# Forgetting attention and a SwiGLU FFN on one core: attention by query block, the FFN fed in 128-token blocks, transposes by DMA, and one planned order for all engines

## The chip, the cores and the metric

The kernel runs on one NeuronCore of a Trainium2 chip. The core has TensorE (PE, matrix products, whose weight loads the profile lists as PEld), VectorE (DVE), ScalarE (ACT), GpSimd (POOL), and SyncE (SP), which here only issues DMAs. Sixteen DMA engines move data between HBM and the on-chip SBUF. Matrix products land in PSUM, which has eight banks of 128 partitions x 512 fp32. The metric is the device time of one execution in microseconds (us); smaller is better.

## The reference, cut to what matters

q, k and v are 8 batches x 8 heads x 576 tokens x 64 in fp32; f is one forget gate per token and head. The FFN weights are 512 x 1536 (gate and value) and 1536 x 512 (out).

```python
scores = scale * np.matmul(q, k.transpose(0, 1, 3, 2))
log_f = np.log(np.clip(f, 0.0001, 1.0))
cum = np.cumsum(log_f, axis=-1)
decay = cum[:, :, :, None] - cum[:, :, None, :]
causal = np.triu(np.ones((S, S), dtype=bool), k=1)
scores = np.where(causal, -1000000000.0, scores + decay)
...
attn = attn / (np.sum(attn, axis=-1, keepdims=True) + 1e-09)
return np.matmul(attn, v).astype(np.float32)
...
xn = x / rms * rms_g
g = xn @ w_gate
silu = g * (1.0 / (1.0 + np.exp(-g)))
val = xn @ w_val
return (silu * val @ w_out).astype(np.float32)
```

x is the attention output with the eight heads side by side: 4608 tokens x 512, so one batch is 576 rows of x, which is four blocks of 128 tokens and one of 64.

## The kernel before

**Attention.** A batch b goes through the same steps. `load_qk` (line 73) issues ten casting DMAs on POOL's queue (fp32 in HBM to bf16 in SBUF; line 77), one per 128-token block of q and of k. `load_v` (line 83) issues five on SP's. `transposes` (line 163) turns q and k on TensorE: per pair of heads five 128x128 transposes into one PSUM tile `tr`, then a DVE copy (line 169); 40 transposes a batch. `scale_v` (line 155) multiplies v by the decay factor on POOL and appends the factor as a 65th column, so that the same product gives the denominator. `scores` (line 194) works head by head: a head's whole causal triangle fills three PSUM banks of 512 columns (`BANKS`), a matmul contracts over 64 rows, head 2p in partitions 0 to 63 and head 2p+1 in 64 to 127, each bank is exponentiated by one ACT instruction of 128x512 (line 205), and POOL masks the diagonals (lines 208 and 213). `scores4` (line 171) does the last 64x64 corner of all heads. `values` (line 225) makes 15 matmuls of 65 columns for a head, all five query blocks, and DVE divides (lines 234 and 235). Only when all eight heads are done are the batch's five blocks of x complete. Then `norm` (line 240) takes the squares on ACT (245), the power on POOL (249), the scaling on DVE (252), and `transpose_x` (line 254) turns the batch's xn in 20 TensorE transposes and copies them into `xT` with the gain (265).

**FFN.** Groups of 512 tokens, so nine groups that straddle batches. `gate(g, fc)` (line 290) does four gate matmuls of 512 columns, tanh on ACT, a DVE product (301), four value matmuls, a second DVE product (306); twelve of these a group. `project(g, j)` (line 308) does twelve matmuls for 128 tokens, an ACT copy and a store on SP; four a group. Three PSUM banks `ff` serve both.

**Order.** Each engine runs its instructions in program order. The loads of weights, of batch 1 and of `wo` are issued behind batch 0's loads, all of batch 0's attention comes first (lines 331 and 332), and then a loop over the FFN's 144 pieces interleaves the attention of batches 1 to 7, by costs written beside each piece, with a lead of six pieces:

```python
for work in ffn:
    n += 1
    want = lead + total_a * n / (slots + LEAD)
    while i < len(stream) and done_a < want:
        done_a += stream[i][0]
        stream[i][1]()
        i += 1
    work[1]()
```

Of the kernel before, what the change touches and what calls it, by code (L numbers as in the profile page):

```python
# [8 lines left out]
F32 = mybir.dt.float32  # L9
# [14 lines left out]
def kernel(  # L24
    ctx: ExitStack,
    tc: tile.TileContext,
    q: bass.AP,
    k: bass.AP,
    v: bass.AP,
    f: bass.AP,  # L30
    moe_w_gate: bass.AP,
    moe_w_val: bass.AP,
    moe_w_out: bass.AP,
    moe_rms_g: bass.AP,
    out: bass.AP,
):
# [4 lines left out]
    NB = 5  # L41
    DM = moe_w_gate.shape[0]
    DF = moe_w_gate.shape[1]
    NDC = DM // 128
    NFC = DF // 128
    GT = 512
    n_grp = B * S // GT
    scale = 1.0 / (D ** 0.5)

    consts = ctx.enter_context(tc.tile_pool(name="consts", bufs=1))  # L50
    ldp = ctx.enter_context(tc.tile_pool(name="ldp", bufs=1))
    vp = ctx.enter_context(tc.tile_pool(name="vp", bufs=6))
    qkt = ctx.enter_context(tc.tile_pool(name="qkt", bufs=2))
    ptp = ctx.enter_context(tc.tile_pool(name="ptp", bufs=5))
    xp = ctx.enter_context(tc.tile_pool(name="xp", bufs=2))
    xnp = ctx.enter_context(tc.tile_pool(name="xnp", bufs=1))
    small = ctx.enter_context(tc.tile_pool(name="small", bufs=4))
    xtp = ctx.enter_context(tc.tile_pool(name="xtp", bufs=3))
    hp = ctx.enter_context(tc.tile_pool(name="hp", bufs=2))
    ep = ctx.enter_context(tc.tile_pool(name="ep", bufs=3))  # L60
    ps_tr = ctx.enter_context(tc.tile_pool(name="ps_tr", bufs=1, space=PSUM))
    ps_sc = ctx.enter_context(tc.tile_pool(name="ps_sc", bufs=3, space=PSUM))
    ps_o = ctx.enter_context(tc.tile_pool(name="ps_o", bufs=1, space=PSUM))
    ps_f = ctx.enter_context(tc.tile_pool(name="ps_f", bufs=3, space=PSUM))


    qb = [ldp.tile([128, NB, H * D], BF16, name=f"qb{i}") for i in range(2)]
    kb = [ldp.tile([128, NB, H * D], BF16, name=f"kb{i}") for i in range(2)]
    Vs = [ldp.tile([128, NB, H, D + 1], BF16, name=f"Vs{i}") for i in range(2)]
    PT4 = [[ldp.tile([128, 5 * 64], BF16, name=f"PT4_{i}{j}") for j in range(2)] for i in range(2)]  # L70


    def load_qk(b):
        for j in range(NB):
            p0, n = j * 128, min(128, S - j * 128)
            for src, dst in ((q, qb[b % 2]), (k, kb[b % 2])):
                nc.gpsimd.dma_start(  # L77
                    out=dst[0:n, j, :].rearrange("p (h d) -> p h d", d=D),
                    in_=src[b, :, p0:p0 + n, :].rearrange("h p d -> p h d"))

    v32s = {}

    def load_v(b):
        for j in range(NB):
            p0, n = j * 128, min(128, S - j * 128)
            v32 = v32s[b, j] = vp.tile([128, H, D], F32, name="v32")
            nc.sync.dma_start(out=v32[0:n, :, :],
                              in_=v[b, :, p0:p0 + n, :].rearrange("h p d -> p h d"))

    fr = consts.tile([BH, S], F32)  # L90
    nc.sync.dma_start(out=fr, in_=f.rearrange("b h s -> (b h) s"))

    for t in qb + kb:
        nc.vector.memset(t[64:128, NB - 1, :], 0.0)
    load_qk(0)
    load_v(0)
    for t in Vs:
        nc.vector.memset(t[64:128, NB - 1, :, :], 0.0)
    for pair in PT4:
        for t in pair:  # L100
            nc.vector.memset(t[:, 4 * 64:], 0.0)

    ident_f = consts.tile([128, 128], F32)
    make_identity(nc, ident_f)
    ident = consts.tile([128, 128], BF16)
    nc.vector.tensor_copy(ident, ident_f)

    rg = consts.tile([128, NDC], F32)
    with nc.allow_non_contiguous_dma(reason="512 gains, once"):
        nc.sync.dma_start(out=rg, in_=moe_rms_g.rearrange("(c p) -> p c", p=128))  # L110
    mhalf = consts.tile([128, NB], F32)
    nc.gpsimd.memset(mhalf, -0.5)


    wg = consts.tile([128, NDC, DF], BF16)
    wv = consts.tile([128, NDC, DF], BF16)
    wo = consts.tile([128, NFC, DM], BF16)

    def load_w(i):
        c0, c1 = i * 512, (i + 1) * 512  # L120
        for w, src in ((wg, moe_w_gate), (wv, moe_w_val)):
            nc.gpsimd.dma_start(out=w[:, :, c0:c1],
                                in_=src[:, c0:c1].rearrange("(c p) f -> p c f", p=128))

    def load_wo():
        for i in range(2):
            nc.gpsimd.dma_start(
                out=wo[:, i * 6:(i + 1) * 6, :],
                in_=moe_w_out[i * 768:(i + 1) * 768, :].rearrange("(c p) f -> p c f", p=128))


    nc.vector.tensor_scalar(fr, in0=fr, scalar1=1e-4, op0=ALU.max, scalar2=1.0, op1=ALU.min)
    nc.scalar.activation(fr, fr, ACT.Ln)
    one = consts.tile([BH, 1], F32)
    nc.vector.memset(one, 1.0)
    ones = bass.AP(tensor=one.tensor, offset=one.offset, ap=[one.ap[0], [0, S]])
    cum = consts.tile([BH, S], F32)
    nc.vector.tensor_tensor_scan(cum, ones, fr, 0.0, ALU.mult, ALU.add)
    mid = consts.tile([BH, 1], F32)
    nc.vector.tensor_tensor(mid, cum[:, 0:1], cum[:, S - 1:S], ALU.add)  # L140
    nc.vector.tensor_scalar_mul(mid, mid, 0.5)
    dec = consts.tile([BH, NB * 128], F32)
    nc.vector.memset(dec[:, S:], 0.0)
    nc.scalar.activation(dec[:, 0:S], cum, ACT.Exp, scale=-1.0, bias=mid[:, 0:1])
    decT = consts.tile([128, NB, BH], F32)
    for j in range(NB):
        dps = ps_o.tile([128, BH], F32, name="po")
        nc.tensor.transpose(dps, dec[:, j * 128:(j + 1) * 128], ident_f[0:BH, 0:BH])
        nc.vector.tensor_copy(decT[:, j, :], dps)


    QT, KT, PT = {}, {}, {}
    xs, xTs = {}, {}

    def scale_v(b):
        for j in range(NB):
            v32 = v32s.pop((b, j))
            n = min(128, S - j * 128)
            dj = decT[0:n, j, b * H:(b + 1) * H]
            nc.gpsimd.tensor_tensor(Vs[b % 2][0:n, j, :, 0:D], v32[0:n, :, :], bcast(dj, D), ALU.mult)  # L160
            nc.gpsimd.tensor_copy(Vs[b % 2][0:n, j, :, D], dj)

    def transposes(b, p):
        for src, store, nm in ((qb[b % 2], QT, "QT"), (kb[b % 2], KT, "KT")):
            tp = ps_tr.tile([128, NB * 128], BF16, name="tr")
# [214 lines left out]
```

## Time and profile before

| what | value |
|---|---|
| time, median of 3 runs | 486.65 us (486.64 to 487.0) |
| span of the profiled execution, first to last instruction | 484.0 us |
| around the span, median less span | 2.65 us |
| busy share PE, DVE, ACT, POOL | 88%, 54%, 46%, 39% |
| granted TensorE clock | 1.000 |
| bytes moved by DMA | 33.73 MB |

The profile shows one execution. The time of that execution outside the span is not listed; the table takes it from the median. A timeline row gives the start, the time that it covers, engine, line, output<-input, shape and count; in brackets stands the idle time of the engine before the row and what released it. Matmuls overlap in the pipeline, so a matmul's own duration (380 ns for 512 columns) is longer than the step from one start to the next; prices are taken from the steps. An SPq row is the time that SP's sequencer spent on issuing a DMA.

### The profile page before, as it was taken

The page shows a single profiled execution, that of the slowest core. Times are in us where ns is not written, and L with a number is a line of the kernel's source. Part 1 is how long each engine was busy: PE and PEld are TensorE (multiplying, and loading weights), DVE is VectorE, ACT ScalarE, POOL GpSimd, SP SyncE. Part 2 cuts the span into 40 slices and gives each one's busy share as a digit, 9 for nine tenths or more (in the row PEclk, how much of TensorE's full clock was granted, in tenths as well). Part 3 has the DMA queues.
Part 4 walks back from the last instruction along what each step waited for, and adds up shares of the span by engine and source line. Part 5 has one row for each costly group of instructions (what it writes and reads, how often), then busy time and mean ns, then how long its engine had stood idle before and what let it go on. Part 6 is the DMA issues. An engine that isn't in the chain of part 4 may idle for free.

```text
span 484.0 us, 8505 instructions
## 1 busy us (share of the span) xinstructions
PE 423.9 (88%) x3317; PEld 207.6 (43%) x3317; DVE 260.3 (54%) x534; ACT 222.1 (46%) x436; POOL 187.7 (39%) x335
## 2 busy tenths in 40 slices
PE   0491707999999999999999999999999999999996
PEld 0231403454544454445444544454444544444442
DVE  3210326478447844784478457745774577373670
ACT  3060321664465437544754474447444744232321
POOL 8539990665182518252825282513111211000000
PEclk9999999999999999999999999999999999999999
DMA  9999991594190419041903290010001000201102
GB/s 151 175 195 178 191 187 33 36 65 99 65 120 3 100 66 119 3 100 67 120 1 77 70 118 0 1 66 23 3 0 66 23 1 0 88 1 45 43 1 87
DMA packets 123080, 33.73 MB, mean 70 GB/s; under 512 B 113760, under 2 KB 118368, under 8 KB 123040
## 3 DMA queue, kind: packets, MB, share of 16 engines
q0 software_dynamic: 79744, 14.16, 36.6%
q1 hardware_dynamic: 43296, 19.03, 14.9%
q8 instruction: 26, 0.43, 0.4%
q14 instruction: 14, 0.11, 0.1%
HBM read 37.90 MB, written 9.44 MB: 98 GB/s over the span
## 4 chain that ended last, share of the span: by engine, by line
PE 67%; POOL 13%; issue 6%; DMA 6%; ACT 5%; DVE 2%; POOLq 0%; ACTq 0%
PE ff L311 20%; PE ff L296 14%; PE ff L304 13%; PE sc L202 7%; PE po L231 5%; PE tr L167 4%; DMA wv<-in_moe_w_val_dram 3%; PE tr L258 3%; POOL Vs_104 L160 2%; DMA qb_100<-in_q_dram 2%; ACT junk L245 2%; POOL Vs_105 L160 2%; POOL rs L249 2%; ACT PT L205 2%; POOL qb_100 L77 2%
## 5 line engine op out<-in xcount | busy, mean ns | idle before, releaser
L205 ACT ACTIVATE PT<-sc 128x512 bf16<-128x512 f32 x192 | 105.1, 599 | 87.6 <-PE sc L202 73.8
L296 PE MATMUL ff<-xT,wg 128*128 128x512 bf16 x432 | 114.7, 382 | 0.7 <-DVE xT L265 0.6
L304 PE MATMUL ff<-xT,wv 128*128 128x512 bf16 x432 | 114.0, 380 | 0.0
L311 PE MATMUL ff<-wo,hT 128*128 128x512 bf16 x432 | 112.5, 380 | 0.0
L301 DVE SCALAR_TENSOR_TENSOR ga<-th,ff 128x512 f32<-128x512 f32 x108 | 74.2, 687 | 66.9 <-ACT th L299 66.3
L299 ACT ACTIVATE th<-ff 128x512 f32<-128x512 f32 x108 | 64.5, 598 | 82.6 <-PE ff L296 80.9
L306 DVE SCALAR_TENSOR_TENSOR hT<-ga,ff 128x512 bf16<-128x512 f32 x108 | 74.2, 687 | 9.0 <-PE ff L304 0.3
L304 PEld LDWEIGHTS <-wv 128*128 128x128 bf16 x432 | 42.2, 98 | 50.2 <-issue 2.5
L208 POOL TENSOR_SCALAR_AFFINE_SELECT PT<-PT 128x128 bf16<-128x128 bf16 x64 | 19.1, 299 | 97.8 <-ACT PT L205 97.6
L296 PEld LDWEIGHTS <-wg 128*128 128x128 bf16 x432 | 38.6, 98 | 42.0 <-issue 5.6
L314 ACT COPY ores<-ff 128x512 f32<-128x512 f32 x36 | 21.1, 586 | 75.2 <-PE ff L311 74.4
L213 POOL TENSOR_SCALAR_AFFINE_SELECT PT<-PT 128x384 bf16<-128x384 bf16 x64 | 33.0, 528 | 53.2 <-ACT PT L205 53.1
L311 PEld LDWEIGHTS <-hT 128*128 128x128 bf16 x432 | 36.5, 98 | 36.4 <-issue 9.5
L231 PEld LDWEIGHTS <-PT 128*128 128x128 bf16 x896 | 35.7, 102 | 31.2 <-POOL PT L208 9.7
L234 DVE RECIPROCAL rden<-po 128x5 f32<-128x5 f32 x64 | 12.2, 191 | 55.3 <-PE po L231 55.3
L258 PE MATMUL tr<-ident,xn 128*128 128x128 bf16 x160 | 20.6, 229 | 18.3 <-DVE xn L252 18.0
L231 PE MATMUL po<-Vs_104,PT 128*128 128x65 bf16 x448 | 22.7, 206 | 13.6 <-POOL PT L208 9.2
L235 DVE TENSOR_TENSOR x<-po,rden 128x320 f32<-128x320 f32 x64 | 31.4, 490 | 1.7
L245 ACT ACTIVATE junk<-x 128x512 bf16<-128x512 f32 x40 | 25.0, 624 | 9.0 <-DVE x L235 8.4
L258 PEld LDWEIGHTS <-xn 128*128 128x128 bf16 x160 | 12.4, 100 | 37.0 <-DVE xn L252 29.1
L265 DVE TENSOR_SCALAR xT<-tr,rg 128x512 bf16<-128x512 bf16 (+7 forms) x64 | 20.5, 362 | 12.3 <-PE tr L258 12.1
L252 DVE TENSOR_SCALAR xn<-x,rs 128x512 bf16<-128x512 f32 x40 | 18.1, 520 | 13.2 <-POOL rs L249 13.2
(300 smaller groups left out, 387.8 us busy)
## 6 DMA issues: line engine op xcount, KB each, us to landing
out_dram<-ores SPq DMA_DIRECT2D x36, 256.0 KB, 2.0
qb_100<-in_q_dram POOLq DMA_DIRECT2D x16, 128.0 KB, 5.3
kb_102<-in_k_dram POOLq DMA_DIRECT2D x16, 128.0 KB, 5.4
qb_101<-in_q_dram POOLq DMA_DIRECT2D x16, 128.0 KB, 4.4
kb_103<-in_k_dram POOLq DMA_DIRECT2D x16, 128.0 KB, 4.5
wg<-in_moe_w_gate_dram POOLq DMA_DIRECT2D x3, 512.0 KB, 12.7
wv<-in_moe_w_val_dram POOLq DMA_DIRECT2D x3, 512.0 KB, 14.0
wo<-in_moe_w_out_dram POOLq DMA_DIRECT2D x2, 768.0 KB, 12.3
```

What stands on the lines that cost most here:

```text
L202: nc.tensor.matmul(sc[:, c:c + n], lhsT=KT[b, p][rows, kj * 128:(kj + 1) * 128], rhs=QT[b, p][rows, q0:q0 + n], start=True, stop=True)
L205: nc.scalar.activation(t[:, bank * 512:(bank + 1) * 512], sc, ACT.Exp, scale=scale)
L213: nc.gpsimd.affine_select(out=d, in_=d, pattern=[[0, 3], [1, 128]], compare_op=ALU.is_ge, fill=0.0, base=0, channel_multiplier=-1)
L231: nc.tensor.matmul(po[:, qi, :], lhsT=weights_of(b, h, qi, kj), rhs=Vs[b % 2][:, kj, h, :], start=(kj == 0), stop=(kj == qi))
L245: nc.scalar.activation(junk, x[:, j, :], ACT.Square, accum_out=sq[:, j:j + 1])
L258: nc.tensor.transpose(tp[:, j * 128:(j + 1) * 128], xn[:, j, dc * 128:(dc + 1) * 128], ident)
L296: nc.tensor.matmul(pg, lhsT=wg[:, dc, fc * 128:(fc + 1) * 128], rhs=xT[:, dc, :], start=(dc == 0), stop=(dc == NDC - 1))
L299: nc.scalar.activation(t, pg, ACT.Tanh, scale=0.5)
L301: nc.vector.scalar_tensor_tensor(a, in0=t, scalar=1.0, in1=pg, op0=ALU.add, op1=ALU.mult)
L304: nc.tensor.matmul(pv, lhsT=wv[:, dc, fc * 128:(fc + 1) * 128], rhs=xT[:, dc, :], start=(dc == 0), stop=(dc == NDC - 1))
L306: nc.vector.scalar_tensor_tensor(hTs[g][:, fc, :], in0=a, scalar=0.5, in1=pv, op0=ALU.mult, op1=ALU.mult)
L311: nc.tensor.matmul(po, lhsT=hTs[g][:, fc, j * 128:(j + 1) * 128], rhs=wo[:, fc, :], start=(fc == 0), stop=(fc == NFC - 1))
```

## The change

The kernel is rewritten around a plan that is made when the program is built. Every piece of work is a `Unit` with an engine, a duration written by hand, a priority key (lower goes first), the units that it depends on and the buffers (`Hold`) that it takes and gives back. `Plan.run` plays the units through in time: whenever an engine is free, the ready unit with the lowest key whose buffers are free starts. The order in which units started is the order in which the instructions are emitted, for all engines. Emission is under `tc.manual_schedule()`.

What the units are:

- **Attention by query block.** A score unit covers one or two tiles of a query block `qi` and a key block `kj`, for all eight heads at once: a tile is two PSUM banks (even heads and odd heads), filled by eight matmuls of 128 columns that alternate between the two row halves, one ACT exponential of 128x1024 and, on the diagonal, one POOL mask of 128x1024. The 64 tokens of the last block take two key blocks to a tile. A value unit is four heads of one query block, with a DVE division behind it. A block of x is complete when its query block is, and not when the batch is.
- **Norm by one or two blocks.** Squares on ACT, power on POOL, and one DVE operation for scale and gain. For batch 0's first four blocks TensorE turns xn, with a DVE copy. All other blocks (36) are turned by a DMA transpose on SP from SBUF to SBUF.
- **q and k.** The first four blocks of batches 0 and 1 are turned on TensorE (64 transposes); the other 64 blocks, each 128 (or 64) tokens x 512, by a DMA transpose on SP.
- **V** is scaled on DVE for batches 0 and 1, and on POOL for the others.
- **FFN.** Group g is now the first 512 tokens of batch g; the ninth is the eight 64-token remainders. Groups 0 and 1 are fed by 128-token blocks: one unit does four columns of fc for one block (16 matmuls of 128 columns for the gate, 16 for the value). The others do as before. The plan splits a projection in three units.
- **Buffers.** PSUM is two score tiles of two banks, one bank for the value product, three for the FFN; `tr` is gone, and once the last score is done its banks go to the FFN.

```diff
-LEAD = 6
+class Plan:
...
+            for eng, line in ready.items():
+                if busy.get(eng) or not line:
+                    continue
+                best = None
+                for u in line:
+                    if best is not None and u.key >= best.key:
+                        continue
+                    want = [h.ring for h in u.take if h.slot is None]
+                    if all(len(free[r]) >= want.count(r) for r in want):
+                        best = u
...
+                order.append(best)
...
+    def load(eng, issue, moves, key, emit, deps=(), take=(), give=()):
+
+        lane = Hold("hw" if eng == "SP" else "sw", 1)
+        u = P.add(eng, issue, key, emit, deps, list(take) + [lane], ())
+        return P.add("DMA", moves, key, None, [u], (), list(give) + [lane], lat=1.7)
...
+    LEAD, SPAN = 0.3, 0.85
+    def akey(b, w):
+        return b - 1 - LEAD + SPAN * w
...
+    load_w(0, -12.5)
+    load_w(1, -11.5)
+    load_w(2, -10.5)
+    load_wo(-9.5)
+    for b in range(B):
         for j in range(NB):
+            key = (-15 + j * 0.5, -10 + j * 0.05)[b] if b < 2 and j < LAST else -9 + b if b < 2 else b - 2.2 + j * 0.1
+            load_qk(b, j, key)
+            load_v(b, j, key + 0.01)
...
+    def turn(b, j, key):
...
+            if b < 2 and j < LAST:
...
+                u = pe(0.25, key, emit, [iden, qkload[b, nm, j]], take=[h], give=[hq])
...
+                def emit(dst=dst, hq=hq):
+                    nc.sync.dma_start_transpose(out=dst[hold_QT[b].slot][:, :, p0:p0 + n],
+                                                in_=T_qk[hq.slot][0:n, :])
+                turned[b, nm, j] = load("SP", 1.3, 1.1, key, emit, [qkload[b, nm, j], zero],
+                                        take=[hold_QT[b]], give=[hq])
...
+    def score_block(tiles, key):
...
+                for i, kj in enumerate(kjs):
+                    for p in range(4):
+                        for par in range(2):
+                            r = slice(par * 64, par * 64 + 64)
+                            c = i * 256 + p * n
+                            nc.tensor.matmul(t[:, par, c:c + n], lhsT=kt[r, p, kj * 128:(kj + 1) * 128],
+                                             rhs=qt[r, p, qi * 128:qi * 128 + n], start=True, stop=True)
...
+        u = pe(0.19 + 0.24 * cols, key, emit, deps, take=holds, give=gives)
...
+                for p in range(4):
+                    for kj in range(qi + 1):
+                        h, c = hold_PT[b, qi, kj]
+                        c += par * 512 + p * n
+                        nc.tensor.matmul(po[:, p, :], lhsT=T_PT[h.slot][:, c:c + 128], rhs=vs[:, kj, 2 * p + par, :],
+                                         start=(kj == 0), stop=(kj == qi))
...
+            if b == 0 and j < LAST:
...
+                def tr(n=n, hn=hn, g=g, c=c):
+                    nc.sync.dma_start_transpose(out=T_of[g][hold_xT[g].slot][:, :, c:c + n],
+                                                in_=T_xn[hn.slot][0:n, :])
+                pieces[b, j] = load("SP", 1.3, 1.1, key, tr, [u], take=[hold_xT[g]], give=[hn])
...
+    order = [(b, qi) for b in range(2) for qi in range(LAST)] + [(0, LAST), (1, LAST)]
+    order += [(b, qi) for b in range(2, B) for qi in range(NB)]
...
+    for g in range(G):
+        if g < 2:
+            for i in range(3):
+                for j in range(4):
+                    hdone.setdefault((g, j), []).append(
+                        gate(g, g + (i * 4 + j) / 16, [pieces[g, j]], i,
+                             [(i * 4 + c, j * 128, 128, c * 128) for c in range(4)]))
+            continue
+        deps = [pieces[g, j] for j in range(4)] if g < B else [pieces[b, LAST] for b in range(B)]
+        us = [gate(g, g + fc / 16, deps, fc // 4, [(fc, 0, GT, 0)]) for fc in range(NFC)]
...
+    with tc.manual_schedule():
+        for u in P.run():
+            if u.emit is not None:
+                u.emit()
```

In `load`, the first figure is the plan's time on the issuing queue and the second its time on the DMA engines; 1.7 is added until the data counts as landed. In `pe`, `act`, `dve` and `pool` the first figure is the unit's duration. Eight DMAs may be out on each of the two issuing queues.

More of the change, by code (lines that the diff above doesn't have):

```diff
@@ L23, with fox_ffn_kernel @@
 @with_exitstack
[L24 to L36, printed above, removed]
+def fox_ffn_kernel(ctx, tc, q, k, v, f, moe_w_gate, moe_w_val, moe_w_out, moe_rms_g, out):
     nc = tc.nc
@@ L90 @@
[L90 to L123, printed above, removed]
@@ L125, in load_wo @@
-    def load_wo():
-        for i in range(2):
[L127 to L149, printed above, removed]
@@ L152 @@
[L152 to L165, printed above, removed]
-            for j in range(NB):
-                nc.tensor.transpose(tp[:, j * 128:(j + 1) * 128], src[:, j, p * 128:(p + 1) * 128], ident)
-            t = store[b, p] = qkt.tile([128, NB * 128], BF16, name=f"{nm}{p}")
-            nc.vector.tensor_copy(t, tp)
```

576 lines of the change are left out of this document (382 added, 194 removed).

## The prediction

> **What bounds the kernel now.** I read the page's busy shares and slices first, then PE's list of waits, then the timeline where PE stands still, last the groups of the other engines.
>
> ```profile
> PE 423.9 (88%) x3317; PEld 207.6 (43%) x3317; DVE 260.3 (54%) x534; ACT 222.1 (46%) x436; POOL 187.7 (39%) x335
> PE   0491707999999999999999999999999999999996
> DMA  9999991594190419041903290010001000201102
> GB/s 151 175 195 178 191 187 33 36 65 99 65 120 3 100 66 119 3 100 67 120 1 77 70 118 0 1 66 23 3 0 66 23 1 0 88 1 45 43 1 87
> PE tr L258 <- DVE xn L252: 18.0, 9, 10.5
> PE po L148 <- POOL ident_f masks.py:199: 11.8, 1, 11.8
> ```
>
> A slice is 12.1 us. For six slices the DMA engines are full and PE mostly waits; from the eighth on PE is full to the end. PE's two largest waits on one line lie wholly or mostly in the start (10.5 of the 18.0 is one wait for batch 0's xn). So there are two costs: the start, and the work that PE does afterwards. The start in the timeline, and PE's last pieces in the chain of waits:
>
> ```profile
> 37.95 1.67 POOL L127 DMA_DIRECT2D wo<-in_moe_w_out_dram  x2
> 40.39 1.04 POOL L160 TENSOR_TENSOR Vs_104<-v_126,decT 128x512 bf16<-128x512 f32 x1
> 46.41 0.29 PE L231 MATMUL po<-Vs_104,PT 128*128 128x65 bf16 x2 [9.19 <-POOL PT L208]
> 75.89 0.58 PE L296 MATMUL ff<-xT,wg 128*128 128x512 bf16 x1 [0.58 <-DVE xT L265]
> ...
> 469.88 10.38 PE ff L311 x48
> ```
>
> POOL issues loads until 39.6 us; only then does it scale V and mask, and batch 0's value products wait 9.19 for it. All of batch 0 must be through before the first gate at 75.9. The last product ends at 480.3, the span at 484.0, so the tail is **3.7**. 48 products in 10.38 are 0.2163 each; 1296 of them are **280.3 us** of FFN, which the change keeps. Between 75.9 and 480.3 lie 404.4 us, so 124.1 go to attention and PE's gaps. In one steady period:
>
> ```profile
> 185.80 0.97 PE ff L296 x4
> ...
> 233.82 0.97 PE ff L296 x4
> ```
>
> The pattern repeats after 48.02 us with 144 FFN products (31.15), so a batch of attention takes **16.9 us of PE**. Its pieces:
>
> ```profile
> 189.23 1.03 PE L304 MATMUL ff<-xT,wv 128*128 128x512 bf16 x4
> 190.19 0.40 PE L202 MATMUL sc<-QT_2003,KT_2011 64*128 64x384 bf16 x4
> 190.52 0.59 PE L231 MATMUL po<-Vs_105,PT 128*128 128x65 bf16 x14
> 190.95 0.19 PE L231 MATMUL po<-Vs_105,PT_10_108 128*128 128x65 bf16 x1
> 190.98 1.02 PE L296 MATMUL ff<-xT,wg 128*128 128x512 bf16 x4
> ...
> 214.21 0.23 PE L258 MATMUL tr<-ident,xn 128*128 128x128 bf16 x1 [0.96 <-DVE xn L252]
> ...
> 221.87 0.44 PE L167 MATMUL tr<-ident,kb_102 128*128 128x128 bf16 x5
> 222.15 0.81 PE L311 MATMUL ff<-wo,hT 128*128 128x512 bf16 x3
> 222.89 0.44 PE L167 MATMUL tr<-ident,qb_100 128*128 128x128 bf16 x5
> 223.26 0.20 PE L177 MATMUL sc<-QT_2648,KT_2656 64*128 64x64 bf16 x2
> ```
>
> Four value products of the FFN from 189.23 cover 0.87, to 190.10. The score pair of two banks starts 0.09 later and takes 0.33, so 0.42 in all. One after the other its 1024 columns would take 0.43 without any gap, so the two row halves run partly at once: 0.22 for 512 columns, and 0.2 to go in and out. A head's 15 value products take 0.46, 30 ns each. Five transposes take 0.28 ahead of an FFN product and 0.37 ahead of a score. By this a batch is 4 transpose groups x 0.37 and 8 x 0.28 = 3.7, 12 score pairs x 0.42 = 5.0, the corner 0.5 (estimate), values 8 x 0.46 = 3.7 and a wait of 1.0: 13.9. **3.0 us** stay unexplained, and I carry them along.
>
> **The change part by part.**
>
> *PE, steady.* Transposes leave PE from batch 2 on (3.7), and the wait for xn with them (1.0). Scores: seven units a batch, 12.5 tiles of eight 128-column products in alternating halves: 7 x 0.2 + 12.5 x 0.22 = 4.1; if the halves ran in series, 12.5 x 0.44 + 1.4 = 6.9. The row above is nearer to the first, and I take it. Values: the same 120 products, 3.7. With the 3.0 that is **10.8 a batch instead of 16.9**, a period of 41.95.
>
> *The cover.* The other engines must fit into 41.95 us. A period of theirs today (busy time of PE, PEld, DVE, ACT, POOL in that order), and single rows:
>
> ```profile
> 186.00:234.00 48.00, 46.83 (x398) 22.96 (x397) 29.48 (x62) 26.00 (x53) 22.59 (x41) 1.00 0.56 72
> L205 ACT ACTIVATE PT<-sc 128x512 bf16<-128x512 f32 x192 | 105.1, 599 | 87.6 <-PE sc L202 73.8 <-POOL PT L208 12.6 <-PE po L231 0.7
> L180 ACT ACTIVATE PT_10_108<-sc 128x256 bf16<-128x256 f32 x4 | 1.5, 384 | 0.4 <-PE sc L177 0.2
> L301 DVE SCALAR_TENSOR_TENSOR ga<-th,ff 128x512 f32<-128x512 f32 x108 | 74.2, 687 | 66.9 <-ACT th L299 66.3
> L235 DVE TENSOR_TENSOR x<-po,rden 128x320 f32<-128x320 f32 x64 | 31.4, 490 | 1.7
> ```
>
> ACT: 256 columns more cost 0.215, so an exponential of 1024 is 1.03; 12.5 of them (13) stand for 24 at 0.6 and two at 0.38 (15): 24 of its 26 stay. DVE loses the copies of turned q, k and xn and gains two divisions and a scaling with two inputs: 24 products at 0.69, ten divisions at 0.6 (0.40 for 256 columns and the reciprocal), five scalings at 0.69, 26. POOL masks the same triangles and makes three powers instead of one: 22.6 and some 3. All stay below 41.95, so no other engine becomes the bound; but ACT's pieces grow from 0.6 to 1.03, and a tanh behind one holds an FFN bank for as long. If that cover fails, the bound is what the attention costs now, 16.9.
>
> *The DMA transposes.* No row shows one; 15 a batch on SP. The nearest rows:
>
> ```profile
> 2.04 0.57 SPq L87 DMA_DIRECT2D v_128<-in_v_dram  x1
> 43.73 5.29 SPq L87 DMA_DIRECT2D v_206<-in_v_dram  x1
> v_1940<-in_v_dram SPq DMA_DIRECT2D x1, 256.0 KB, 3.0
> kb_102<-in_k_dram POOLq DMA_DIRECT2D x16, 128.0 KB, 5.4
> ```
>
> An issue takes SP 0.57 with free DMA engines and 5.29 with full ones; a load lands after 3.0 to 5.4. If each transpose held SP for t, a period would be at least 15t + 5 (five v loads and four stores); below t = 2.4 PE covers it. The DMA engines are busy some 17 of 48 us today (slices 1, 9, 0 and 4 tenths), so they would carry up to 1.7 a transpose; 128 KB at the 180 GB/s of the start are 0.7. I take t near the free issue row, up to the 1.3 that the plan writes down: no cost. Queued behind a waiting transpose are stores and v loads; with three `ores` buffers a stuck SP stops ACT's copies and then PE's FFN bank. The transposes' keys stand 0.25 of a group, some 10 us, ahead of the scores, which covers landing times like those above.
>
> [...]
>
> *The start.* POOL makes the identity first, batch 0's q and k in blocks, then weights; V goes to DVE. When can FFN work begin? Rows of a turned copy and of the weights:
>
> ```profile
> 22.80 0.49 DVE L169 COPY QT_234<-tr 128x640 bf16<-128x640 bf16 x1 [0.65 <-PE tr L167]
> 10.56 0.76 POOL L122 DMA_DIRECT2D wg<-in_moe_w_gate_dram  x1 [0.33 <-DMA qb_100<-in_q_dram]
> 19.28 15.89 DMA wv<-in_moe_w_val_dram
> wg<-in_moe_w_gate_dram POOLq DMA_DIRECT2D x3, 512.0 KB, 12.7
> ```
>
> The last gate weights land at 35.2 now and stand at the same place in the queue. The first are issued at 10.6; at the 12.7 that such a load takes there, and the value weights a little later, gates can start at about 24. Then DVE is full: memsets 4.3 (plan), V 8 x 0.75 (plan; a product of that size is 0.69), q and k copies 16 x 0.4, 16 divisions 9.6, four scalings and copies 4.4, group 0's products 24 x 0.69 = 16.5, together 47.6 from about 12 us. So at **59 us** group 0's gates and four blocks of batches 0 and 1 are done. DMA: the first six slices moved 13 MB; 9.4 MB (weights, two batches) take 53 us at that rate, so DMA doesn't set a later end. Bounds: 50 (weights alone) and 85 (POOL's DMA waits in front of masks, as at 40 us now).
>
> *Sum.* 59; FFN left, 280.3 less 96 products (20.8) plus 0.9 for group 1's extra loads, 260.4; attention 6 x 10.8 and the last blocks of batches 0 and 1, 2.2 each, 69.2; tail 3.7: a span of 392.3. Around the span lie 2.65 (486.65 less 484.0, the span being of one profiled execution): **395 us**.
>
> **The rivals.**
>
> *The start stays long (85).* For it: POOL is one queue, and masks stand behind DMA issues that wait for a free lane. Against: the plan orders both by time. 395 + 26 = 421.
>
> *Attention costs PE what it does now.* An order fixed at build time stalls where true latencies differ, and longer exponentials hold tanh back. 6 x (16.9 - 10.8) = 37: 432.
>
> *Transposes bind a little.* With t = 3.0, the landing of a v load, the period is 50: 395 + 6 x 8.05 = 443.
>
> *Slower: transposes in a row.* If they don't overlap and each holds its queue for t = 5.4 (kb's landing), a period is 86 and the time 395 + 6 x 44 = 659. It turns slower where 6 x (15t + 5 - 41.95) passes 91.7, at t = 3.5. For it: SP issues in order, and stood 5.29 on one issue under load. Against: in the steady part the DMA engines are idle for more than half of the slices.
>
> **How the numbers follow.** Forecast 395: 62%, own range 372 to 412 (a start of 50 and little of the 3.0, or a start of 70 and scores half in series). Long start 421: 12%. No gain in attention 432: 9%. Transposes bind 443: 8%. Slower: 9%. The range takes in all but the last: 372 to 443. A measurement tells 0.2%, about 1 us, from no change. Faster 90%, same 1%, slower 9%.
>
> **What would show it.** Right: first gate near 24 us, PE full from 60, a steady period near 42, PE's waits below 1 us each, transposes landing within 4 us. Wrong: SP's list of waits led by transposes, scores waiting for DMA `KT`, or a start in which PE waits for POOL's masks. My sum fails first if a DMA transpose costs over 2.4 us of SP or 1.7 of the DMA engines.

## The result and the profile after

| what | before | after |
|---|---|---|
| time, median of 4 runs | 486.73 us (486.64 to 487.0) | 414.09 us (408.07 to 415.02) |
| ratio to before, 95% interval | | 0.8444 (0.8381 to 0.8506) |
| profiled execution: time; span | not listed; 484.0 us | 414.21 us; 412.5 us |
| first gate product | 75.9 us | 31.1 us |
| steady period (144 FFN products) | 48.02 us | 39.5 us |

The ratio leaves out the two of the four runs that took over 1.5% longer than the fastest, the profiled one among them, so it stands nearer to 411 than to 414 us. The differences between kernels below are differences of such ratios times 486.7. The forecast was 395 (372 to 443).

Page of the kernel after: busy times, the slices of 10.3 us each, two DMA queues (packets, MB, share of 16 engines' span), median landing times, and two groups.

```profile
PE 363.5 (88%) x3831; PEld 215.0 (52%) x3877; DVE 249.1 (60%) x478; ACT 209.4 (51%) x332; POOL 176.9 (43%) x255
PE   0469795899897999889999999999999989999995
PEclk9988999899999799989999999999999999999999
DMA  9999999989999949979999983310131020101104
q0 software_dynamic: 79744, 14.16, 47.2%
q1 hardware_dynamic: 91232, 30.84, 42.5%
QT<-qk SPq DMA_TRANSPOSE x32, 4.7
KT<-qk SPq DMA_TRANSPOSE x32, 4.2
xT<-xn SPq DMA_TRANSPOSE x28, 4.2
L382 ACT ACTIVATE PT<-sc 128x1024 bf16<-128x1024 f32 x96 | 95.1, 1021 | 45.7 <-PE sc L366 44.7 <-POOL PT L390 0.7
L458 DVE SCALAR_TENSOR_TENSOR xn<-x,rs,rgb 128x512 bf16<-128x512 f32 (+1 forms) x40 | 39.6, 1006 | 0.5 <-POOL rs L451 0.5
```

PE's busy time fell by some 60 us, at the same share of the span. (The trace of the change lacks the records of 46 matmuls, 3831 against 3877 weight loads, all behind 80 us; so PE's busy time is a little too low there.) The slices show two halves: up to slice 18, 186 us, PE has holes and the granted clock dips; behind it PE is full. The DMA engines are full, but for single slices, until about 247 us (two of the expectations below say 260) and mostly idle from then on. Before, they were full for 72 us only.

The end of the chain of waits, for the steady part; in between stand pieces of the same pattern:

```profile
5.24 13.81 DMA qk<-in_q_dram
...
21.97 21.82 DMA qk<-in_q_dram
...
48.40 14.85 DMA qk<-in_q_dram
...
63.34 7.93 DMA QT<-qk
...
196.63 3.56 PE ff L519 x16
...
237.21 3.56 PE ff L519 x16
...
276.73 3.56 PE ff L519 x16
...
316.24 3.56 PE ff L519 x16
```

The pattern returns after 40.58, 39.52 and 39.51 us. Less 144 products (31.15), attention with PE's gaps takes **8.4 us of PE a batch**; before it took 16.9. Of the first 71 us of the chain 58 are DMA: three loads of q and one transpose.

PE's timeline through the early part (start, time covered, line, shapes, count; in brackets the idle time before):

```profile
29.98 0.61 PE L467 MATMUL ff<-ident,xn 128*128 128x128 bf16 x4 [0.44 <-DVE xn L458]
...
31.10 1.86 PE L519 MATMUL ff<-xT,wg 128*128 128x128 bf16 x16
...
43.83 0.40 PE L319 MATMUL ff<-ident,qk 128*128 128x128 bf16 x4 [1.48 <-DMA qk<-in_q_dram]
...
71.31 0.83 PE L366 MATMUL sc<-QT,KT 64*128 64x64 bf16 x32 [3.03 <-DMA QT<-qk]
...
75.09 1.96 PE L519 MATMUL ff<-xT,wg 128*128 128x128 bf16 x32
...
133.93 1.87 PE L519 MATMUL ff<-xT,wg 128*128 128x512 bf16 x4 [2.83 <-issue]
...
176.03 1.02 PE L519 MATMUL ff<-xT,wg 128*128 128x512 bf16 x4 [1.84 <-DMA xT<-xn]
```

Counted in FFN products of 512 columns (four of 128 columns count as one), the row at 75.09 brings PE to 96, as many as group 0's gates have: 76.8 us. 432 products, three groups' worth, are through at 185.9. These two marks are used for all kernels below; they are the starts of the 96th and the 432nd product's weight load, since no weight load is missing. (The expectations below name some second marks 2 to 3 us earlier, 183 and 173.) Between them and after them (windows: length, busy time of PE, PEld, DVE, ACT, POOL with counts, granted clock; then the DMA engines' share and GB/s):

```profile
31.00:76.80 45.80, 37.36 (x692) 34.50 (x690) 32.09 (x75) 25.26 (x40) 25.25 (x35) 0.93 1.74 169
76.80:185.90 109.10, 99.56 (x1302) 65.17 (x1313) 65.30 (x125) 63.18 (x102) 75.60 (x108) 0.95 1.25 143
185.90:265.00 79.10, 76.65 (x750) 39.96 (x763) 54.15 (x98) 48.10 (x78) 44.40 (x64) 1.00 1.18 136
134.00:141.00 7.00, 6.78 (x46) 3.42 (x47) 1.89 (x4) 3.63 (x6) 1.33 (x2) 0.58 1.34 225
```

PE idles 8.4 us in the first window, 9.5 in the second and 2.5 in the third; 11 and 13 matmul records are missing from the last two, so these two figures are upper bounds. The second also ran at 0.95 of the clock, which is 5.5 us of 109.1. The last row shows a place: around the wait that ends at 133.93 the clock is granted at half (0.50 from 133.0 to 139.8 us, 0.58 in the mean of the row). What PE waits for there, by the chain, is the DMA transpose of xn:

```profile
125.69 7.00 DMA xT<-xn
```

### The profile page after: what moved, and what is told of

Read it like the earlier page. It is cut to its first block, busy times and chain, and to the rows that moved or that the text cites. A ratio compares the mean times of both kernels' runs of the same rounds, so it can differ in the third digit from the quotient of the medians.

```text
span 412.5 us, 9584 instructions
## 1 busy us (share of the span) xinstructions
PE 363.5 (88%) x3831; PEld 215.0 (52%) x3877; DVE 249.1 (60%) x478; ACT 209.4 (51%) x332; POOL 176.9 (43%) x255
## 3 DMA queue, kind: packets, MB, share of 16 engines
q0 software_dynamic: 79744, 14.16, 47.2%
q1 hardware_dynamic: 91232, 30.84, 42.5%
## 4 chain that ended last, share of the span: by engine, by line
PE 59%; DMA 19%; POOL 8%; DVE 7%; issue 6%; ACT 1%; POOLq 0%; ACTq 0%; DVEq 0%; SPq 0%
PE ff L519 26%; DMA qk<-in_q_dram 12%; PE ff L543 12%; PE sc L519 6%; PE po L414 5%; PE sc L543 4%; DMA xT<-xn 4%; PE sc L366 4%; POOL qk L266 3%; DVE xn L458 2%; DVE ga L532 2%; DVE hT L526 2%; DMA QT<-qk 2%; POOL Vs L343 2%; POOL PT L390 1%
## 5 line engine op out<-in xcount | busy, mean ns | idle before, releaser
L382 ACT ACTIVATE PT<-sc 128x1024 bf16<-128x1024 f32 (+1 forms) x104 | 99.8, 988 | 52.9 <-PE sc L366 51.7
L519 PE MATMUL ff<-xT,wv 128*128 128x128 bf16 (+1 forms) x636 | 91.0, 286 | 3.9 <-DVE ga L532 2.4
L519 PE MATMUL ff<-xT,wg 128*128 128x128 bf16 (+1 forms) x616 | 85.4, 283 | 5.7 <-issue 2.8
L519 PEld LDWEIGHTS <-wg 128*128 128x128 bf16 x720 | 54.2, 99 | 43.3 <-issue 5.2
L390 POOL TENSOR_SCALAR_AFFINE_SELECT PT<-PT 128x1024 bf16<-128x1024 bf16 x32 | 35.1, 1096 | 77.5 <-ACT PT L382 77.4
L414 PE MATMUL po<-Vs,PT 128*128 128x65 bf16 x960 | 44.7, 197 | 8.7 <-DVE x L430 6.0
L458 DVE SCALAR_TENSOR_TENSOR xn<-x,rs,rgb 128x512 bf16<-128x512 f32 (+1 forms) x40 | 39.6, 1006 | 0.5 <-POOL rs L451 0.5
L428 DVE RECIPROCAL rden<-po 128x4 f32<-128x4 f32 (+1 forms) x80 | 14.2, 177 | 42.2 <-PE po L414 41.9
L266 POOL DMA_DIRECT2D qk<-in_k_dram x40 | 34.7, 867 | 8.3 <-DMA wv<-in_moe_w_val_dram 5.3
L366 PE MATMUL sc<-QT,KT 64*128 64x128 bf16 (+1 forms) x960 | 35.1, 218 | 3.5 <-DMA QT<-qk 3.0
L343 POOL TENSOR_TENSOR Vs<-v,decT 128x512 bf16<-128x512 f32 (+1 forms) x30 | 32.7, 1089 | 10.8 <-PE po L414 10.7
L266 POOL DMA_DIRECT2D qk<-in_q_dram x40 | 35.6, 890 | 1.2 <-issue 0.7
L366 PEld LDWEIGHTS <-KT 64*128 64x128 bf16 x960 | 25.6, 99 | 19.7 <-issue 17.8
L430 DVE TENSOR_TENSOR x<-po,rden 128x256 f32<-128x256 f32 (+1 forms) x80 | 33.8, 423 | 2.8
```

The costliest lines, as they stand in the source:

```text
L266: nc.gpsimd.dma_start(out=T_qk[h.slot][0:n, :].rearrange("p (h d) -> p h d", d=D), in_=src[b, :, p0:p0 + n, :].rearrange("h p d -> p h d"))
L343: eng.tensor_tensor(T_Vs[hv.slot][0:n, j, :, 0:D], T_v32[h.slot][0:n, :, :], bcast(dj, D), ALU.mult)
L366: nc.tensor.matmul(t[:, par, c:c + n], lhsT=kt[r, p, kj * 128:(kj + 1) * 128], rhs=qt[r, p, qi * 128:qi * 128 + n], start=True, stop=True)
L382: nc.scalar.activation(T_PT[hp.slot][:, 0:1024].rearrange("p (a c) -> p a c", a=2)[:, :, 0:cols], T_sc[h.slot][:, :, 0:cols], ACT.Exp, sca ...
L390: nc.gpsimd.affine_select(out=d, in_=d, pattern=[[0, 8], [1, n]], compare_op=ALU.is_ge, fill=0.0, base=0, channel_multiplier=-1)
L414: nc.tensor.matmul(po[:, p, :], lhsT=T_PT[h.slot][:, c:c + 128], rhs=vs[:, kj, 2 * p + par, :], start=(kj == 0), stop=(kj == qi))
```

## The experiments

Each edit is to the kernel after, if nothing else is said. The times are medians, with the ratio to before and its interval.

**q and k of all batches turned on PE** (blocks of 128; the 64-token ones stay on DMA).

```diff
-            if b < 2 and j < LAST:
+            if j < LAST:
```

> q and k of all batches are turned on TensorE (four blocks of each batch; the 64-token block stays a DMA transpose): 48 blocks more. TensorE theory: 48 x 0.25 us more of PE and nothing saved, so 12 us slower than the changed kernel, 420 to 427 us. DMA theory (the DMA engines are full from 0 to 260 us of the changed kernel, and the transposes are part of it): with 48 transposes gone loads land earlier and the time stays or falls, 400 to 412 us.

435.16 us, 0.8931 (0.8898 to 0.8965): 24 us slower than the change. Neither theory has the size. The second mark came at 194.3 instead of 185.9, and the next three times 144 products took 47.1, 42.2 and 41.7 us instead of 39.2, 41.1 and 38.9. PE's own attention work rose by only 1.8 a batch (eight groups of four transposes at 0.23 each); the rest is waiting, and PE's list now has DVE in it, which gained the 48 copies:

```profile
PE ff L543 <- DVE hT L526: 4.1, 2, 3.8
PE ff L519 <- DVE ga L532: 4.1, 2, 3.1
```

So the transposes of q and k by DMA bring more than the PE time that they free. A second cost was left out of both theories: a block that is turned on PE takes one of the three FFN banks (`take=[h]`, with `Hold("ff", 1)`) until DVE has copied it, and DVE's products `ga` and `hT` give such banks back. How the extra splits between banks, DVE and the clock stays open.

**xn of all batches turned on PE.**

```diff
-            if b == 0 and j < LAST:
+            if j < LAST:
```

> xn of batches 1 to 7 is turned on TensorE and copied by DVE, 28 blocks. Landing theory (groups 2 and 3 start late because the DMA transpose of xn lands late, PE idles 2.8 and 1.8 us and then runs at a granted clock of 0.5 for one or two stretches of 3.4 us): 6.5 us more of PE, but the waits and the half-clock stretches after 80 us go, so about even, 406 to 413 us, with a granted clock of 1.00 from 80 us on. Rival (those waits come from something else): 6.5 us slower, 417 to 421 us, the low clock stays.

416.34 us, 0.8561 (0.8513 to 0.8609), some 6 us slower. 432 products were through at 175.9, 10 us earlier than in the change, and the clock line has a single dip:

```profile
PEclk9999996999999999999999999999999999999998
```

Then it was given back: the next three times 144 products took 43.1, 41.3 and 40.4 instead of 39.2, 41.1 and 38.9. So turning xn by DMA costs time up to the second mark and saves it behind.

**Groups 0 and 1 fed with 512 columns, like the others.**

```diff
-        if g < 2:
+        if g < 0:
```

> Groups 0 and 1 take whole 512-token groups like the others instead of 128-token blocks. Theory: the start is bound by what DMA brings and by DVE, so the first gate comes some 9 us later but the end of group 0's gates moves by less than 4 us: 411 to 417 us. Rival (the block feed is what shortens the start): all 9 us show, 420 us and more.

413.76 us, 0.8484 (0.8439 to 0.8528): the same as the change. The first gate came at 47.7 instead of 31.1, and 200 products at 117.9 instead of 108.6; but 432 at 184.1 against 185.9. The gain of the block feed is lost again by then; in the change the wait for group 2's xT and the half clock lie in between.

**The ten memsets of PT as ten units**, so that others can go between them.

```diff
-    zero2 = dve(3.5, -8, emit_zero2)
+    zero2 = [dve(0.57, -8, lambda t=t: nc.vector.memset(t, 0.0)) for t in T_PT]
```

> The one 5.7 us block of memsets that stands on DVE in front of the decay chain is split into ten units that the plan can place between urgent ones. DMA theory (the first weights land at 27 to 30.5 us and bound the first gate at 31.1): 0 to 2 us faster, first gate still after 29 us, 408 to 413 us. DVE theory (the decay chain bounds the start): 4 to 6 us faster, first gate near 26 us.

407.11 us, 0.8366 (0.8339 to 0.8394). The first gate stayed at 31.1. The two marks came at 75.1 and 180.1, so most of the gain lies between them, where PE idled 6.0 us instead of up to 9.5 and the granted clock was 0.98 instead of 0.95:

```profile
75.10:180.10 105.00, 99.00 (x1345) 64.69 (x1343) 65.94 (x127) 64.61 (x104) 76.63 (x108) 0.98 1.40 149
```

Its interval overlaps that of the change (0.8381 upward) at the edge, and the change's own best run was 408.07: whether the order helps or the clock fell better isn't told apart.

**The same, and xn on PE for batches 0 to 2 only.**

```diff
-            if b == 0 and j < LAST:
+            if b <= 2 and j < LAST:
```

> xn of batches 1 and 2 only is turned on TensorE, and the memsets are split as in e4_split_memset. Theory: turning xn on TensorE pays where the DMA engines are full (group 2 waits for the DMA transpose of xn; with all xn on TensorE 432 FFN products were through at 173 us instead of 183) and costs later, where they are free (periods of 41 to 43 us instead of 39.5). So the early gain without the later cost: 398 to 403 us, 432 products through by 172 us. Rival (the early gain is given back whatever comes later): 406 us as e4_split_memset.

406.43 us, 0.8347 (0.8322 to 0.8371). The marks: 85.2 and 179.5. The time of the kernel with split memsets, as the rival had it: 10 us late at the first mark, level at the second. The first mark isn't like for like: PE had done 40 score and 60 value products and 16 transposes more by then, some 4 us at the steps above.

**The four products of one row half in a row**, instead of alternating halves.

```diff
-                    for p in range(4):
-                        for par in range(2):
+                    for par in range(2):
+                        for p in range(4):
```

> The eight score products of a tile are issued first for the even heads, then for the odd ones, instead of alternating between the two row halves. Theory (products in the two halves run at once only when they are neighbours in the queue): a tile takes 0.44 us instead of 0.22, 12.5 tiles x 8 batches, 22 us slower, 428 to 436 us, of which some hides in the start. Rival (order does not matter): 408 to 414 us.

411.42 us, 0.8472 (0.8427 to 0.8516): the same, and so the rival. A score unit of two tiles and the row behind it, first of the change, then of this kernel:

```profile
98.62 0.62 PE L366 MATMUL sc<-QT,KT 64*128 64x128 bf16 x16
99.17 0.30 PE L414 MATMUL po<-Vs,PT 128*128 128x65 bf16 x4
```

```profile
212.71 0.64 PE L366 MATMUL sc<-QT,KT 64*128 64x128 bf16 x16
213.28 0.30 PE L414 MATMUL po<-Vs,PT 128*128 128x65 bf16 x4
```

0.55 and 0.57 from one start to the next. 2048 columns in series would take 0.87 at 0.2163 for 512. So the halves overlap in both orders; why the order doesn't matter stays open.

**1.5 MB of loads more at the head of SP's queue** (six blocks of v, into buffers that are overwritten before they are read).

```diff
+    for i, t in enumerate(T_ores + T_th + T_ga[:1]):
+        load("SP", 0.6, 1.2, -14.8, lambda i=i, t=t: emit_more(i, t))
```

> Six more loads of v blocks (1.5 MB, not used) at the head of SP's queue. DMA theory (until 75 us the DMA engines are what everything waits for): 1.5 MB at 170 GB/s are 9 us, so the end of group 0's gates moves from 76.8 to 84 to 87 us and the time by 6 to 10 us, 418 to 423 us. Rival (DVE, ACT and POOL chains set the start): under 3 us, 409 to 414 us.

417.77 us, 0.8579 (0.8538 to 0.862): 6.6 us slower, or 4.2 us a MB (six times 256 KB). PE waited 14.9 in one piece for batch 0's first xn:

```profile
PE ff L474 <- DVE xn L465: 14.9, 1, 14.9
```

The first gate came at 44.9 instead of 31.1, but the first mark at 79.0 instead of 76.8, with 3 us of attention left undone. So traffic in the start costs, though less than the bare transfer (9 us at 168 GB/s); the DMA theory had the total nearly right and the mark wrong.

**Each transpose of a 128-token block of q and k from batch 2 on issued twice**, the second into a tile that nobody reads; 48 DMAs more, order unchanged.

```diff
+                    if b >= 2 and j < LAST:
+                        nth[0] += 1
+                        nc.sync.dma_start_transpose(out=dummy[nth[0] % 4], in_=T_qk[hq.slot])
```

> Every DMA transpose of a 128-token q or k block of batches 2 to 7 is issued twice, the second time into a tile that nobody reads: 48 more, 58 us more of SP's issue time at 1.2 us, the plan's order unchanged. Cover theory (SP has 24 of 39.5 us in use): at most 4 us slower, 409 to 417 us. DMA theory (the engines are full from 75 to 260 us, so each transpose delays a load): 10 to 25 us slower, 422 to 438 us.

447.52 us, 0.92 (0.9174 to 0.9225): 37 us slower, more than either theory. Page and PE's waits:

```profile
DMA  9999999999999989969997998542013011101104
q1 hardware_dynamic: 117344, 37.13, 47.8%
```

```profile
PE ff L523 <- DMA xT<-xn: 18.9, 4, 8.1
```

SP's queue moved 6.29 MB more, and its packets took 47.8% of 444.2 less 42.5% of 412.5, which is 37 us more: **0.77 us of packet time on the 16 DMA engines a transpose** (131 KB). Packets in flight together are each counted in full (the DMA share in the windows above goes up to 1.74), so this is an estimate from above. That the kernel lost 37 us too doesn't show that it lost them there. Up to the second mark (201.5 instead of 185.9), with the engines full, it lost 16. The rest went behind it: the next two times 144 products took 45.0 and 51.2 us before they fell to 39.0, and the longest wait there comes while SP, and not the DMA engines, is full:

```profile
285.57 1.89 PE L523 MATMUL ff<-xT,wg 128*128 128x512 bf16 x4 [7.18 <-DMA xT<-xn]
```

```profile
279.15 1.22 SPq L330 DMA_TRANSPOSE QT<-qk  x1
280.42 1.26 SPq L334 DMA_TRANSPOSE dm<-qk  x1
281.77 2.53 SPq L481 DMA_TRANSPOSE xT<-xn  x2
```

The xn of that group was scaled by 272.4. Its transposes were issued at 281.77, because SP issued others of q and k without a pause from 267.8 on; the slice from 277.6 on has the DMA engines at 5 tenths. So the late part is lost in SP's queue. Of the early part the trace leaves open whether the DMA engines or SP's queue bind.

**The kernel before, with q and k of batches 1 to 7 turned by DMA.** Ten transposes a batch on SP, in place of the 40 on PE and their copies; the pieces' cost in the interleaving is 0 instead of 0.6, so the order shifts a little too.

```diff
+                    for j in range(NB):
+                        nc.sync.dma_start_transpose(out=store[b][:, :, j * 128:(j + 1) * 128], in_=src[:, j, :])
+                continue
-            a.append((0.6, lambda p=p: transposes(b, p)))
+            a.append((0.6 if b == 0 else 0.0, lambda p=p: transposes(b, p)))
```

> One part alone: the kernel before, with q and k of batches 1 to 7 turned by ten DMA transposes a batch on SP in place of 40 on TensorE; everything else as it was. TensorE theory: eight groups of five at 0.28 to 0.37 us, 2.6 us a batch, less over seven batches, 18 us faster: 463 to 472 us; the DMA engines are idle for more than half of that time and cover it. Rival (SP issues in order, the transposes stand behind stores that wait for FFN results, and the scores wait for them): 480 us or more.

507.81 us, 1.0452 (1.0413 to 1.0492): slower than before, as the rival had it. PE's busy time fell from 423.9 to 409.1, and the waits took it back. PE's list, then SP's:

```profile
PE tr L265 <- DVE xn L259: 30.9, 9, 14.2
PE sc L184 <- DMA KT<-kb: 15.4, 2, 8.7
```

```profile
SPq L323 <- ACT ores L321: 244.5, 36, 33.7
SPq L171 <- DMA qb<-in_q_dram: 33.6, 5, 24.6
```

SP stood up to 24.6 us on a transpose whose block had not landed, and up to 33.7 on stores that waited for ACT (32.7 in the kernel before). Much the same transposes that bring 24 us in the planned order cost 22 here.

**The plan with one duration, 0.6, for every unit** (all dependencies and keys as they are).

```diff
-        u = Unit(eng, dur, key, emit, lat)
+        u = Unit(eng, 0.6, key, emit, lat)
```

> The changed kernel with every duration of the plan, those of the DMA engines too, set to 0.6 us; keys, buffers and latencies stay. Theory (the plan needs true durations to place attention between FFN products and loads between masks): 10 us slower or more, 421 to 450 us. Rival (keys and buffers alone set a good order): 406 to 417 us.

453.26 us, 0.9326 (0.9282 to 0.9369): 43 us slower, more than the theory's. The first gate came at 61.7, the marks at 105.7 and 216.7. The durations written by hand are worth more than half of the change's gain.

**The memsets split, xn of batches 0 to 2 and all of q and k of batches 0 and 1 on PE**, the 64-token blocks too.

```diff
-            if b < 2 and j < LAST:
+            if b < 2:
...
-                        nc.tensor.transpose(tp[:, p * 128:(p + 1) * 128], T_qk[hq.slot][:, p * 128:(p + 1) * 128],
-                                            ident)
+                        nc.tensor.transpose(tp[:, p * 128:p * 128 + n], T_qk[hq.slot][0:n, p * 128:(p + 1) * 128],
+                                            ident[0:n, 0:n])
...
-            if b == 0 and j < LAST:
+            if b <= 2 and j < LAST:
```

> e5_xn_pe_early, and the 64-token blocks of q and k of batches 0 and 1 turned on TensorE too, so that no DMA transpose stands in the start. Theory (PE idles 3.0 us at 71 us for such a transpose, which landed 7.9 us after its issue, and then runs 3.4 us at half clock): 3 to 5 us faster than e5_xn_pe_early, 401 to 404 us. Rival (what is won in the start is given back where loads set the pace): 405 to 408 us.

407.95 us, 0.839 (0.8374 to 0.8407). The marks: 83.0 and 178.9. The 3.03 of waiting for QT is gone, and the gain is given back, as the rival had it: it is 2 us slower than the kernel with xn of batches 0 to 2 on PE. Between its marks PE hardly idles and has the full clock, so there PE's own work is all that is left:

```profile
83.00:178.90 95.90, 94.13 (x1211) 60.76 (x1209) 63.48 (x118) 59.83 (x94) 70.35 (x98) 1.00 1.54 160
```

**That kernel with groups 0 and 1 fed wide** (`if g < 0:` as above).

> e11_start_on_pe with whole 512-token groups for groups 0 and 1. Theory (the 128-token feed gains nothing that stays, as e3_wide_feed was as fast as the changed kernel): equal to e11_start_on_pe within 3 us. Rival (with the start freed the feed pays): 5 us slower than it or more.

415.92 us, 0.8547 (0.8523 to 0.857): 8 us slower than with blocks, the second mark at 187.9. So the block feed does pay where xn comes from PE up to batch 2; in the change its gain is lost on the way to the second mark, and the wait for group 2's xT with the half clock behind it is the likely place.

The fastest are the kernel with split memsets and the one with xn of batches 0 to 2 on PE besides, which can't be told apart; the second lies below the change by 1% with intervals that don't meet.

## Why the prediction was right, point by point

The median lies 2 us above the forecast's own range (372 to 412) and well inside the wide one. Span 412.5 against 392.3: 20.2 more. 17.8 of it is the start (76.8 instead of 59). What lies behind takes 335.7 instead of 333.3, and that is two errors which cancel by luck: attention 6 x (8.4 - 10.8) = -14.6, the tail +1.2 (4.9, from the last copy at 407.6), and +15.8 that the sum didn't have. The window from 76.8 to 185.9 shows most of those: up to 9.5 idle and 5.5 of clock, of which some 3 are the gaps that the 8.4 has in it already.

Of the signs that the prediction gave, the period (39.5 for 42) came as said. The first gate (31.1 for 24), PE full from 60 (186), waits below 1 us (up to 3.03) and landing within 4 us (4.2 to 4.7 in the median, 6.7 to 8.7 for the first seven) did not.

*What bounds the kernel: right.* The gain came from the two places that the prediction named, the start and PE's attention work.

*The start, 59: the step that failed.* The sum let the gates begin when the first weights are there, at 24, and let DVE be full from 12 us on, with everything that it needs at hand. The weights did come: the load issued at 10.81 landed after 13.3, at 24.1. (The row behind the prediction's 35.2 for the last gate weights is one of the value weights.) But the first gate came at 31.1, behind PE's transpose of xn at 29.98, which waited for DVE's scaling; the chain of x was late by 7.1 us. And DVE was not full: it was busy for 53.0 of the 76.8 us and idle for 24. Its work was sized about right (the terms add up to 47.2 and not 47.6), but the blocks of batch 1 were not there. They stand behind the weights in POOL's queue:

```profile
10.81 0.76 POOL L284 DMA_DIRECT2D wg<-in_moe_w_gate_dram  x1 [2.02 <-DMA qk<-in_q_dram]
...
42.08 0.87 POOL L266 DMA_DIRECT2D qk<-in_k_dram  x1 [3.19 <-DMA wv<-in_moe_w_val_dram]
```

```profile
48.31 0.39 SPq L275 DMA_DIRECT2D v<-in_v_dram  x1
```

By the chain the first of batch 1's q blocks was issued at 21.97 and landed 21.82 later, at 43.8; the last k block, issued at 42.08, landed after 7.8, at 49.9. So the turning, scores and exponentials of batch 1 could only begin at 43.8, and the sum has no term for that. In PE's time the 17.8 is 7.1 for the late first gate, and behind it 8.4 of idle time and some 3.2 of clock (0.93 of 45.8) in the first window; these come to 18.7, since PE's work itself was a little less than the 35 us that the sum left for it.

"DMA doesn't set a later end" held for the blocks that it was said of: they had landed by 49.9, before the 53. The queues did run ahead, with batch 2 loaded in the start too. But its first load is the row at 48.31, so it delayed neither the first gate nor batch 1's first four blocks. What it may have delayed lies behind that; PE's longest wait there is the 3.03 for the QT of a 64-token block. That an earlier place in the queue for batch 1 would shorten the start is argued from the landing times; no run changed that order. The run with 1.5 MB more shows only that traffic there costs, 4.2 us a MB.

The rival of the long start (85) came nearer to 76.8 than the forecast did. Its reason is seen in part: in the first 76.8 us POOL stood 14.0 us in all on DMA issues that waited for earlier loads to land. But PE waited for a mask only once, for 1.08; what stood behind POOL's waits was above all the next loads.

*PE's attention, 10.8: too dear by 2.4.* Most of the 3.0 that was unexplained and carried along isn't there: without it the sum was 7.8, and 8.4 was measured, with PE's gaps. Where it sat in the old order isn't known; a residue that belongs to no piece should have been a bound and not a term. The score price (halves partly overlapping) was right: 0.55 for a two-tile unit, where the terms gave 0.64.

*The cover by the other engines: right in the steady part.* The exponential of 1024 took 1.021 (1.03 by the sum). The scaling with two inputs from SBUF took 1.006 in the mean and not 0.69, 1.6 us of DVE a batch that the cover hid: DVE is busy 54.2 of 79.1. (Half of them took 0.75 or less; the mean comes from those beside which POOL worked, see below.) The rival "attention costs PE what it does now" is out.

*The DMA transposes: right in price, wrong in where they are free.* SP's rows:

```profile
66.90 1.34 SPq L329 DMA_TRANSPOSE QT<-qk  x1
...
125.69 3.58 SPq L477 DMA_TRANSPOSE xT<-xn  x2
```

1.2 us of issue in the median (two in 3.58 where it waits, single ones up to 4.22), half of the limit of 2.4, and 0.77 of packet time on the DMA engines where the estimate was 0.7 and the limit 1.7. Landing takes 4.2 to 4.7, a little over the 4 named. SP's list of waits is led by stores that wait for ACT:

```profile
SPq L551 <- ACT ores L548: 76.6, 21, 17.7
```

From 186 us on PE waits for no transpose any more, as forecast, though the DMA engines stay full until about 247. Before that PE's waits are not below 1 us: 3.03 for QT at 71.31, 2.83 at 133.93 where group 2 begins, 1.84 for xT at 176.03. So the rival "transposes bind a little" is partly true, in the start and for two batches, and by late landing, not by SP's issue. With twice the transposes SP's queue binds as well (the wait of 7.18 above). 131 KB in 0.77 us are 170 GB/s, where the estimate took the 180 of the start.

*Slower: transposes in a row.* Its mechanism is real, its point not reached: in the old order SP did stand on a transpose, for up to 24.6 us, and the kernel got slower. That the plan keeps it away here is argued: with all durations equal the kernel lost 43 us, but how much of it to SP isn't known.

*What stays open:* which part of the change's spread from 408 to 415 is the clock, where the extra wait of the kernel with q and k on PE comes from, and why the row halves overlap in either order. No run has the attention by query block without the plan, so how the 8.4 instead of 16.9 splits between the new shape of the work and its order isn't shown.

## What to carry to other kernels

In a start, ask for each piece of work when its inputs land, and not only whether the bytes and the engines' work fit: here the bytes fitted, and DVE still idled for 24 us, while batch 1's blocks stood behind the weights. (No run moves them up.) Work moved to the DMA engines takes time in two places, on them and in the issuing queue (here 0.77 us of packet time and 1.2 us of SP's issue a transpose), and either can be the one that is short: with twice the transposes PE stood 7.18 us while SP was full and the engines were at 5 tenths. Count both in each stretch. Whether DMA transposes paid here hung on the order: much the same ones brought 24 us in the planned order and cost 22 in the old one, where SP stood up to 24.6 us on one whose block had not landed. An earlier start counts only if the next group is ready as well: the block feed was 9.3 us ahead at 200 products and 1.8 behind at 432.

## What the runs showed of the hardware

- Half clock around waits of 1.84 to 3.03 us. The profile of the change has four stretches at a granted clock of 0.50 before the end: 6.8 us from 27.2 on, 3.4 from 71.6, 6.8 from 133.0 and 3.4 from 177.4. PE's waits of 2.28 (to 26.42), 3.03 (to 71.31) and 1.84 us (to 176.03) end 0.8, 0.3 and 1.4 us ahead of the first, second and fourth; the third begins 0.9 us before the end of the wait of 2.83 (to 133.93). Behind the waits of 1.08 to 1.51 that end at 43.83, 65.93, 79.30, 111.16 and 333.01 the clock stayed at 1.00. What sets it isn't shown. A matmul of 512 columns steps by 0.43 instead of 0.22 in the stretch at 133.0; if PE has work all along, a stretch of 3.4 us costs 1.7 (estimate). A run of the change with a mean clock of 0.976 took 413.97 us, one with 0.987 408.07, but one with 0.985 415.02: the clock is not all of the spread. The kernel before had a mean of 1.000, but the granted clock doesn't show all of it: it stands at 1.00 from 76 to 79 us too, where products of 512 columns step by 0.43 (76.80 to 77.23), and PE is back at 0.22 only from 79.6 us on.
- The scaling of x (128x512 or 64x512, two fp32 inputs in SBUF) took 0.75 us on DVE in the median. 13 of the 40 took 1.08 to 2.26: 12 beside work of POOL, 0.45 us of it or more, and one (1.08) beside two of its DMA issues. None of the other 27 took more than 0.81; 21 of them had no work of POOL beside them, eight of these a DMA issue. The product with one input in PSUM took 0.67 to 0.69 always. One of the long ones:

```profile
249.40 1.09 POOL L390 TENSOR_SCALAR_AFFINE_SELECT PT<-PT 128x1024 bf16<-128x1024 bf16 x1 [1.69 <-ACT PT L382]
...
249.56 1.47 DVE L458 SCALAR_TENSOR_TENSOR xn<-x,rs,rgb 128x512 bf16<-128x512 f32 x1
```

- Two row halves of PE overlap whether they alternate or come four in a row: 2048 columns took 0.55 and 0.57 us, where 0.87 is the time in series at 0.2163 for 512.
